# Sorted block attention with a ResMLP on one core: SyncE in program order, mixing of k and v moved to ScalarE half a batch earlier, paired scores, v sort in five pieces

## The chip, the cores and the metric

The kernel runs on one core of a Trainium2 chip. The metric is device time in microseconds (us) for one execution; less is better. The engines are named as in the profile: PE (TensorE, matmuls), PEld (its weight loads), DVE (VectorE), ACT (ScalarE), POOL (GpSimd) and SP (SyncE, which here only issues DMAs and DMA transposes). A line number such as L65 refers to the kernel before.

## The reference

Four batches of attention with 8 heads, 768 tokens and 64 channels a head feed a ResMLP block of width 512. Keys and values are mixed across 8 blocks of 96 tokens by a matrix P, made from `sort_net` by five rounds of normalisation. Attention then stays inside each block.

```python
P = sort_net
for _ in range(5):
    P = P - np.max(P, axis=-1, keepdims=True)
    P = np.exp(P)
    P = P / (np.sum(P, axis=-1, keepdims=True) + 1e-09)
    P = P / (np.sum(P, axis=-2, keepdims=True) + 1e-09)
k_sorted = np.einsum('bhij,bhjcd->bhicd', P, k_b)      # v_sorted the same
scores = scale * np.matmul(q_b, k_sb.transpose(0, 1, 2, 4, 3))
attn = softmax(scores)                                 # per block of 96
x = np.matmul(attn, v_sb)                              # to (batch, 768, 512)
a1 = alpha1 * x + beta1
tok = np.einsum('ts,bsd->btd', w_tok, a1)
u = x + lam * tok
a2 = alpha2 * u + beta2
ch = np.maximum(a2 @ w_ch1, 0.0) @ w_ch2               # 512 -> 2048 -> 512
return u + lam * ch
```

## The kernel before

**Stages.** Each batch runs in two halves (`hf`) of 384 tokens. A half has an "h" phase, the first FFN product, of 16 units of four 128x384 matmuls with a relu on ACT after each (`h_unit`, L739), and a "c" phase, the second product, of three token groups in four parts of four 128x512 matmuls (`ch_unit`, L758). The whole kernel after its head is the loop over batch, half, h units and c parts at L933 to L942. I write a place in it as (batch, half, phase slot), for instance (1,0,c4).

**What is hung beside the slots.** All other work (attention for the next batch, the token product, loads) is attached to these slots by `put` (L859) and carried out by `run` after the slot's matmuls. The table is written at L866 to L920. So PE's order is written out by hand, as a long row of FFN matmuls with pieces of the next batch in between. For batches 2 and 3, called b with p = b − 1, the places are:

- `mix_v` (L534), which mixes the values by `bigM`: (p,0,h8), h9 and h10, each two 128x512 matmuls and a copy of 1024 columns to `mixed` by DVE.
- `bounce_v` (L569) and `back_v` (L575), which write the mixed values to a scratch in DRAM (`vscr`) and gather them back into `Vs` with tokens on partitions: (p,0,h10) and (p,0,c0). Both are DMAs on SyncE.
- `mix_k` (L549), eight matmuls and four copies of 64x512 into `kT`: (p,0,h15), c1 and c4, by DVE, ACT, DVE.
- `q_cross` (L514), six DMA transposes of q on SyncE: listed at (p,0,h11). Batch 1 has `q_turn_late` (L521) in its place, which transposes on PE.
- `score` (L417), eight 96-row matmuls and an exp on ACT, and `pv` (L479), eight matmuls by `Vs`, then a reciprocal and a product on DVE: one at a time from (p,0,c8) to (p,1,h11). The first affine of a finished piece is put on the list `late` (L503) and carried out by `flush` at the next `pv`.
- `tails` (L509), which rearranges the last token rows: (p,1,h12).
- `moe_tok` (L697), the token product with u and its 16-bit copy: the first three pieces all at (p,1,c3), the others at (b,0,h0), h2 and h4. `moe_cross` (L707), three DMA transposes of u to `uT` on SyncE: (p,1,c3) and (b,0,h4). `moe_affine` (L714), which makes `a2T` from `uT` on DVE: (p,1,c7) and (b,0,h13).
- loads of the batch after next on POOL's queue (`load_kv`, `load_q`): (p,0,c11); `mix_matrix` for batches 2 and 3: (0,1,c9) and (1,1,c9).

**The head.** Before the loop (L788 to L850) batch 0 is done with other forms. k is mixed and turned on PE (`k_turn`, `k_copy`). v is rearranged in SBUF by `v_sort` (L162) into `VD`, in four pieces of 16 channels: two on DVE, one each on ACT and POOL; each `v_mix` (L401) needs eight channels. Then come scores, `pv_first` (L453), the token product (`first_mm`) and `first_turn` (L659), which ends with a matmul of one row, `rrow` by `brow`, a rank-1 term of the bias. `first_back` (L676) has three such. `fill` and `warm` (L223, L227) issue matmuls on zeros. `mgap` (L822) fills a padding column range of `Vs[0]`.

**What sets the order.** `Engine` (L55) hands each instruction to its engine and keeps it in program order; since it issues everything at L65, the profile names lines of PE, DVE, ACT and POOL as L65 and one tells them apart by tile. SyncE's DMAs are issued directly (L517, L571, L576, L710, L777, L778) and a scheduler places them: the uT transposes stand behind those of q there. PSUM pool `psA` has two buffers (scores, pv, mixing), `psB` four (FFN and token products). `qn`, `qT`, `mixed` and `u16` have one buffer, `raw` and `kT` two.

## Time and profile before

| | us |
|---|---|
| median of 5 runs | 271.66 (271.05 to 272.94) |
| profiled execution | 271.66 |
| its span on the core | 269.9 |

The granted PE clock is 1.00 of full speed over the span. The span is cut into 40 slices of 6.75 us in the page's second part; a digit is the busy share in tenths:

```profile
ACT  3577766325886003453674003453583014505600
POOL 8767205401671185303560825303100837032000
DMA  6999999999999953249399952159200323112012
GB/s 104 207 203 193 207 207 217 187 141 191 133 182 168 118 118 93 44 117 155 80 185 165 112 143 63 39 125 149 82 0 0 80 58 78 22 39 78 0 41 78
```

ACT goes to zero or near it in every second product, since its work is the relu of the first. DMA traffic is dense for the first 95 us and light later.

SyncE's own list around the end of the first batch, start and duration of each group of issues:

```profile
53.94 3.91 SPq L710 DMA_TRANSPOSE uT<-u  x3
58.92 1.15 SPq L571 DMA_DIRECT2D vscr<-mixed  x2
63.16 0.35 SPq L777 DMA_DIRECT2D out_dram<-ost  x1
63.56 0.40 SPq L778 DMA_DIRECT2D out_dram<-ost  x1
64.47 0.33 SPq L576 DMA_DIRECT2D Vs<-vscr  x1
```

These are the u transposes of half 1 of batch 0, the bounce of batch 1's values, an output store, and the gather of those values.

### The profile page before, as it was taken

Reading aid. Unit: us, or ns where it says so; the run is one execution under the profiler, and the core shown is the slowest. Engines: PE = TensorE matmul, PEld = TensorE weight load, DVE = VectorE, ACT = ScalarE, POOL = GpSimd, SP = SyncE. Lnnn points to the kernel's source line nnn. Section 1 sums busy time; section 2 is a strip of 40 time slices with the busy share of each in tenths; the row PEclk is TensorE's granted clock in tenths of the full one; section 3 lists DMA queues with packets and bytes.
Section 4 is the critical chain, followed back from the end, with each engine's and each line's share of the span. In section 5 each row is a group of like instructions: output and inputs, shape, how many; then the busy total and the mean of one; then the engine's idle time right before and its main releaser. Section 6 shows DMA issues by size and latency. Waiting matters only on the chain.

```text
span 269.9 us, 5367 instructions
## 1 busy us (share of the span) xinstructions
PE 256.3 (95%) x2151; PEld 138.8 (51%) x2165; DVE 175.1 (65%) x363; ACT 116.2 (43%) x220; POOL 98.4 (36%) x104
## 2 busy tenths in 40 slices
PE   7978999999999999999999979999999999999993
PEld 3456665455555444554555435554565445545552
DVE  5798957978378968676778728666878765121032
ACT  3577766325886003453674003453583014505600
POOL 8767205401671185303560825303100837032000
PEclk9999999999999999999999999999999999999999
DMA  6999999999999953249399952159200323112012
GB/s 104 207 203 193 207 207 217 187 141 191 133 182 168 118 118 93 44 117 155 80 185 165 112 143 63 39 125 149 82 0 0 80 58 78 22 39 78 0 41 78
DMA packets 67372, 31.04 MB, mean 115 GB/s; under 512 B 56642, under 2 KB 63058, under 8 KB 67348
## 3 DMA queue, kind: packets, MB, share of 16 engines
q0 software_dynamic: 26352, 15.34, 40.9%
q1 hardware_dynamic: 40900, 15.30, 32.5%
q8 instruction: 17, 0.28, 0.4%
q14 instruction: 7, 0.06, 0.1%
q10 hardware_dynamic: 96, 0.07, 0.1%
HBM read 32.79 MB, written 8.65 MB: 154 GB/s over the span
## 4 chain that ended last, share of the span: by engine, by line
PE 76%; DVE 11%; DMA 7%; issue 3%; POOL 1%; SPq 1%; DVEq 0%; POOLq 0%
PE h_ps L65 29%; PE ch_ps L65 24%; PE tok_ps L65 10%; DMA v<-in_v_dram 4%; DVE a L65 4%; PE x_ps L65 4%; DVE x L65 3%; PE sc_ps L65 2%; DVE ost L65 2%; DMA uT<-u 2%; PE kmix_ps L65 1%; PE v_ps L65 1%; PE mix_ps L65 1%; DVE vd L65 1%; DMA out_dram<-ost 1%
## 5 line engine op out<-in xcount | busy, mean ns | idle before, releaser
L65 PE MATMUL h_ps<-a2T,W1p 128*128 128x384 bf16 x512 | 96.1, 326 | 2.0 <-DVE a2T L65 2.0
L65 ACT ACTIVATE hTa<-h_ps 128x384 bf16<-128x384 f32 x96 | 46.9, 493 | 93.2 <-PE h_ps L65 93.1
L65 POOL TENSOR_TENSOR ost<-ost,u 128x512 f32<-128x512 f32 x21 | 26.6, 1266 | 114.6 <-DVE ost L65 108.2
L65 PE MATMUL ch_ps<-W2p,hTa 128*128 128x512 bf16 (+1 forms) x287 | 67.3, 370 | 0.6
L65 PEld LDWEIGHTS <-W1p 128*128 128x128 bf16 x512 | 47.2, 98 | 34.2 <-issue 3.5
L65 PEld LDWEIGHTS <-hTa 128*128 128x128 bf16 x300 | 28.4, 98 | 29.0
L65 DVE TENSOR_TENSOR ost<-ch_ps,lamB 128x512 f32<-128x512 f32 (+1 forms) x25 | 16.7, 669 | 37.7 <-PE ch_ps L65 34.5
L65 ACT ACTIVATE et<-sc_ps 96x768 f16<-96x768 f32 (+1 forms) x32 | 25.9, 809 | 12.9 <-PE sc_ps L65 12.9
L65 POOL TENSOR_TENSOR u<-toktmp,x 128x512 f32<-128x512 f32 x18 | 29.1, 1633 | 5.1 <-DVE toktmp L65 5.1
L65 PE MATMUL tok_ps<-a,w_tokT 128*128 128x512 f16 x126 | 29.7, 379 | 0.1
L65 PE MATMUL ch_ps<-W2p,hTb 128*128 128x512 bf16 (+1 forms) x99 | 24.8, 370 | 0.1
L65 DVE TENSOR_TENSOR toktmp<-tok_ps,lamB 128x512 f32<-128x512 f32 x21 | 14.4, 687 | 9.6 <-PE tok_ps L65 8.3
L65 DVE TENSOR_TENSOR u<-toktmp,x 128x512 f16<-128x512 f32 (+1 forms) x24 | 19.5, 824 | 0.7
L65 PEld LDWEIGHTS <-w_tokT 128*128 128x128 f16 x126 | 12.2, 98 | 14.3 <-issue 0.6
L65 ACT ACTIVATE hTb<-h_ps 128x384 bf16<-128x384 f32 x32 | 15.7, 490 | 8.0 <-PE h_ps L65 7.6
L65 POOL DMA_DIRECT2D qn<-in_q_dram x18 | 16.0, 913 | 6.2 <-DMA raw<-in_v_dram 6.2
L65 DVE CAST kT<-kmix_ps 64x512 f16<-64x512 f32 x20 | 14.2, 711 | 4.5 <-PE kmix_ps L65 3.0
L65 DVE TENSOR_TENSOR x<-x_ps,rcb 96x512 f16<-96x512 f32 x24 | 16.5, 687 | 0.8
L65 DVE TENSOR_SCALAR a2T<-uT,ab2col 128x384 bf16<-128x384 f16 x28 | 10.4, 434 | 9.3 <-DMA uT<-u 9.3
L65 PE MATMUL x_ps<-Vs,et 96*128 96x65 f16 (+4 forms) x288 | 14.4, 195 | 2.1 <-DVE x L65 1.2
L65 PEld LDWEIGHTS <-et 96*128 96x128 f16 (+4 forms) x288 | 12.5, 100 | 7.0 <-DVE x L65 2.8
L65 ACT CAST kT<-kmix_ps 64x512 f16<-64x512 f32 x16 | 11.4, 714 | 9.7 <-PE kmix_ps L65 9.5
(116 smaller groups left out, 241.7 us busy)
## 6 DMA issues: line engine op xcount, KB each, us to landing
out_dram<-ost SPq DMA_DIRECT2D x23, 192.0 KB, 2.2
raw<-in_v_dram POOLq DMA_DIRECT2D x6, 384.0 KB, 8.0
raw<-in_k_dram POOLq DMA_DIRECT2D x6, 384.0 KB, 10.3
qn<-in_q_dram POOLq DMA_DIRECT2D x18, 128.0 KB, 10.6
vscr<-mixed SPq DMA_DIRECT2D x6, 384.0 KB, 3.7
Vs<-vscr SPq DMA_DIRECT2D x3, 768.0 KB, 7.6
W1p<-in_moe_w_ch_dram POOLq DMA_DIRECT2D x4, 512.0 KB, 13.1
W2p<-in_moe_w_ch_dram POOLq DMA_DIRECT2D x4, 512.0 KB, 17.5
```

The lines of the kernel that those rows point to most:

```text
L65: ins = getattr(self.eng, name)(*args, **kwargs)
```

## The change

- SyncE's DMAs also go through `Engine`, so SyncE issues in the order in which the program lists them.
- For batches 2 and 3, `mix_v` and `mix_k` move half a batch ahead, into the second product of (p−1,1): mix_v at c1, c2, c3, mix_k at c4, c6, c8, all copies by ACT; bounce at c4, gather at c10. Their q transposes are listed at (0,1,h13) for batch 2 and (1,1,h8) for batch 3; in the built program they stand on SyncE behind the stores of the half before.
- Scores and pv of batches 2 and 3 come in pairs: at (p,0,h15), c1, c3, c6, c8, c11, (p,1,h1), h4. `flush` runs one slot after a pv pair and takes the list from its front.
- tails at h8; moe_tok at c0, c1, c2, moe_cross at c2, moe_affine at c6.
- Loads of batch 3 at (1,0,c0); `mix_matrix` at (0,0,c6) and (1,0,h12). q turns of batch 1 stay where they are.
- The head: v sort as ACT 8 + 8 channels, DVE 16, POOL 16 + 16; `brow` and `rrow` become 128 rows, zero but for row 0, so that the rank-1 matmuls run over 128 rows; two fills in `score` go, warm counts 4 and 2 become 3 and 3; the `mgap` copy moves ahead of the k copies; three copies change between DVE and ACT.

```diff
+    sp = Engine(nc.sync)
...
+    brow = att.tile([128, C], F16, name="brow", tag="uT", bufs=2)
+    rrow = att.tile([128, 384], F16, name="rrow", tag="uT", bufs=2)
...
+    dve.memset(brow[:].bitcast(FT), 0.0)
+    dve.memset(rrow[:].bitcast(FT), 0.0)
...
-    def v_sort(n, eng):
...
+    def v_sort(lo, hi, eng):
+        eng(VD[:, lo:hi, 0:HB], v8[:, :, lo:hi].rearrange("p t d -> p d t"))
...
-    v_sort(3, pool.tensor_copy)
+    v_sort(16, 32, pool.tensor_copy)
     for g in range(4):
+        if g == 1:
+            v_sort(48, 64, pool.tensor_copy)
         pool.dma_start(W1p[:, :, g * 512:(g + 1) * 512], w1v[:, :, g * 512:(g + 1) * 512])
-    brow = att.tile([1, C], F16, name="brow", tag="uT", bufs=2)
-    rrow = att.tile([1, 384], F16, name="rrow", tag="uT", bufs=2)
-    pool.tensor_tensor(brow[:], bet1[:], lam1[:], ALU.mult)
+    pool.tensor_tensor(brow[0:1, :], bet1[:], lam1[:], ALU.mult)
...
-        if b == 0 and g == 3:
-            fill(ps[:, 0, :], 1)
...
-        flush()
+        if b == 1:
+            flush()
...
-            late.pop()()
+            late.pop(0)()
...
-        nc.sync.dma_start_transpose(
+        sp.dma_start_transpose(
             qT_of[b][:, :, kt * 128:(kt + 1) * 128], qn_of[b][:, kt, :, :].rearrange("p h d -> p (h d)"),
         )
...
-    warm(4)
+    warm(3)
     mix_values(0, psb)
     prep_scales()
+    dve.tensor_copy(Vs[0][:, :, D:GRP], mgap[:].unsqueeze(2).to_broadcast([128, H * NB, GRP - D]))
...
-    warm(2)
+    warm(3)
...
-    v_sort(0, copy)
+    v_sort(0, 8, act.copy)
+    v_sort(8, 16, act.copy)
     score(0, 0, 0, psa)
     k_copy(0, 3, kp3, 0, copy)
-    k_copy(0, 3, kp3, 1, act.copy)
+    k_copy(0, 3, kp3, 1, copy)
     score(0, 0, 1, psa)
-    v_sort(1, copy)
+    v_sort(32, 48, copy)
...
-    v_sort(2, act.copy)
...
+    pairs = [("s", 0), ("s", 2), ("p", 0), ("s", 4), ("p", 2), ("s", 6), ("p", 4), ("p", 6)]
...
+            for n in range(3):
+                put(p - 1, 1, "c", 1 + n, lambda b=b, n=n: mix_v(b, n, act.copy))
+                put(p - 1, 1, "c", 4 + 2 * n, lambda b=b, n=n: mix_k(b, n, (act.copy,) * 4))
+            put(p - 1, 1, "c", 4, lambda b=b: bounce_v(b))
+            put(p - 1, 1, "c", 10, lambda b=b: back_v(b))
+            for kt in range(NT):
+                put(p - 1, 1, "h", (13 if b == 2 else 8), lambda b=b, kt=kt: q_cross(b, kt))
+            if b + 1 < B:
+                put(p, 0, "c", 0, lambda b=b: load_kv(b + 1), lambda b=b: load_q(b + 1))
+            for (kind, n), at_ in zip(
+                pairs, ((0, "h", 15), (0, "c", 1), (0, "c", 3), (0, "c", 6), (0, "c", 8), (0, "c", 11), (1, "h", 1), (1, "h", 4)),
+            ):
+                if kind == "p":
+                    put(p, at_[0], at_[1], at_[2] + 1, flush)
+                for i in range(2):
+                    f = (lambda b=b, n=n + i: score(b, n // 2, n % 2, psa)) if kind == "s" else (lambda b=b, n=n + i: pv(b, n // 2, n % 2))
+                    put(p, *at_, f)
...
-            put(p, 1, "c", 4 if b == 1 else 3, lambda b=b, kt=kt: moe_tok(b, kt, psb))
-        put(p, 1, "c", 4 if b == 1 else 3, lambda b=b: moe_cross(b, 0))
-        put(p, 1, "c", 8 if b == 1 else 7, lambda b=b: moe_affine(b, 0))
+            put(p, 1, "c", 4 if b == 1 else kt, lambda b=b, kt=kt: moe_tok(b, kt, psb))
+        put(p, 1, "c", 4 if b == 1 else 2, lambda b=b: moe_cross(b, 0))
+        put(p, 1, "c", 8 if b == 1 else 6, lambda b=b: moe_affine(b, 0))
```

The other SyncE calls (`bounce_v`, `back_v`, `moe_cross`, the output stores) change from `nc.sync` to `sp` in the same way as `q_cross`.

## The prediction

> **What bounds the kernel now.** I read the page's busy shares first, then the chain of waits, then PE's own waits, and last the timeline around each stall.

> ```profile
> PE 256.3 (95%) x2151; PEld 138.8 (51%) x2165; DVE 175.1 (65%) x363; ACT 116.2 (43%) x220; POOL 98.4 (36%) x104
> PE 76%; DVE 11%; DMA 7%; issue 3%; POOL 1%; SPq 1%; DVEq 0%; POOLq 0%
> PE h_ps L65 <- DVE a2T L65: 2.0, 2, 1.7
> PE v_ps L65 <- DVE vd L65: 1.4, 1, 1.4
> ```

> PE (first line) is busy for 95% of the span and carries 76% of the chain, so only two things save time: fewer or cheaper matmuls, and fewer PE stalls. The last two lines (us in total, times, longest) name the largest stalls after the start-up. Busy time overstates PE's work: modelled matmul ends overlap, and a matmul held by its operand looks longer. I therefore price stalls by start-to-start distances. Lines from PE's timeline, by place:

> ```profile
> 18.91 0.90 PE L65 MATMUL v_ps<-bigV,vd 64*64 64x64 f16 x32 [1.36 <-DVE vd L65]
> 24.96 1.02 PE L65 MATMUL x_ps<-Vs,et 128*128 128x65 f16 x24 [0.60 <-DVE Vs L65]
> 32.23 0.33 PE L65 MATMUL turn_ps<-rrow,brow 1*128 1x384 f16 x1
> 62.13 0.50 PE L65 MATMUL qt_ps<-ident,qn 128*128 128x128 f16 x6
> 101.27 1.19 PE L65 MATMUL h_ps<-a2T,W1p 128*128 128x384 bf16 x4 [0.29 <-DVE a2T L65]
> 127.68 0.34 PE L65 MATMUL sc_ps<-qT,kT 64*128 64x96 f16 x8
> 127.95 1.04 PE L65 MATMUL ch_ps<-W2p,hTa 128*128 128x512 bf16 x4
> 134.26 0.43 PE L65 MATMUL x_ps<-Vs,et 96*128 96x65 f16 x8 [0.49 <-DVE x L65]
> 161.53 1.19 PE L65 MATMUL h_ps<-a2T,W1p 128*128 128x384 bf16 x4 [1.71 <-DVE a2T L65]
> ```

> Read: two waits in the head (18.91, 24.96), two at the entry of a half's first FFN product (101.27, 161.53), one on a late softmax division (134.26). SyncE's list shows why a2T is late:

> ```profile
> 86.15 8.34 SPq L517 DMA_TRANSPOSE qT<-qn  x6
> 95.67 3.81 SPq L710 DMA_TRANSPOSE uT<-u  x3
> 146.63 8.20 SPq L517 DMA_TRANSPOSE qT<-qn  x6
> 156.02 3.83 SPq L710 DMA_TRANSPOSE uT<-u  x3
> ```

> Six q transposes hold SyncE for 8.3 us right ahead of the uT transposes that a2T needs.

> [...] 156 GB/s at 52 to 56 us, mostly POOL's loads, and 125 at 56 to 60.5 once SyncE's bounce runs too. [...] the same 128x768 v copy on DVE took 2.12 us beside POOL's 1.49 us copy and 0.81 us later. [...] the exps took 0.81. [...]

> **The change, part by part** (against the profiled span 269.9; the run took 271.66, 1.76 outside the span, and equals the median).

> *1. Head.* The v sort in five pieces puts two half pieces on ScalarE [...], one full on DVE, two on POOL. The first v_mix waited 1.36. ScalarE's half piece can be ready 17.6 to 17.9, v having landed at 16.64; but the exps queue behind two pieces, and scores have two PSUM buffers. I give −0.7 here and −0.3 for later v-mix evictions. Moving the 0.49 us gap copy of Vs to an idle stretch of DVE removes the x_ps wait, −0.6. So batch 0's first x_ps starts near 23.4 instead of 24.96. The gap copy now delays the first k copies by 0.49; if the later warm matmul didn't cover this, a third of the head's gain would be lost. The dropped fills (0.33, 0.31) count nothing: there x evictions on DVE set the pace. Four rank-1 turns get 128 rows instead of one; the one-row matmul took 0.27 start to start and slows its neighbour. I estimate 0.2 each, −0.8 (bounds 0 and −1.2); three in first_back, −0.45 (0 to −0.6). The two added memsets run in DVE's idle start. Natural lead before q's turn: 1.6 + 0.8 + 0.45 = **2.85**.

> *2. What the lead meets.* q_turn of batch 1 needs its q pieces. The last load was issued at 50.77 and took 9.5 us: landed 60.2. POOL's queue is busy with weights and loads throughout the head (about 205 GB/s), so a faster PE doesn't bring it forward. Worse, SyncE's uT transposes (53.94) and the 768 KB bounce (58.92, 3.7 us) move up by the lead, beside that q. If the bounce takes its whole time ahead of q, q lands at 63.9, 1.8 us behind today's turn; if it costs nothing, the whole lead passes. I take 61.5, PE's turn at 61.6 instead of 62.13: **−0.5** (bounds +1.8, −2.85).

> *3. uT stalls.* At 101.27 PE lost 0.47 idle plus 0.38, because the first four h matmuls took 1.03 instead of 0.65 while a2T pieces came: 0.85. At 161.53: 1.88 + 0.38 = 2.26. Sum **3.1**. After: mix_v and mix_k for batches 2 and 3 move into the preceding (p−1, 1) second product, about 1.3 + 1.35 us of PE work, which moves PE's arrival 2.65 later relative to this chain; batch 3's q transposes go onto SyncE some 8 us sooner, tok matmuls up to three slots sooner. Batch 2's q transposes still stand ahead of uT(1,0) (about 86 to 94), but a2T is only needed near 102. New in-order waits on SyncE: behind a held q transpose stand an output store, uT and then the v bounce; q of batch 2 is loaded a phase ahead, and its buffer is free when the last score of batch 1 is done, as now. Bound if in-order SyncE still holds uT: gain 0. I take −3.1. ScalarE's new load in that product: [...] 12 x 0.714 (kT row) [...], where it was busy for 0.38 and 0.50. The last copy ends about 1.8 after the phase; the first relu result is needed about 3.2 after. That cover is 1 to 2 us; without it each us late is a us on PE, twice.

> *4. Late softmax division.* 133.60 to 134.26 = 0.66, once each for batches 2 and 3: **−1.3**. DVE loses its mix copies there and pv's are further apart. In a pair the second waits for a PSUM buffer instead; the slots leave about 4 us between pairs, and exp (0.81 x 2) or division (about 1.1 x 2) fits. Bounds 0, −1.3.

> *5. Pairs.* A single score costs 0.27 start to start at 127.68, and stretches the next ch group by about 0.1 [...]: 0.38. A pair: about 0.45 + 0.10. Saved 0.2 x 8 pairs = **−1.6** (bounds 0, −2.4).

> Sum −0.5 − 3.1 − 1.3 − 1.6 = −6.5: span 263.4, time **265.2**. PE's matmul work otherwise stays; the earlier batch-3 loads (about 112 instead of 132) run in a stretch of light DMA use.

> **Rivals.** (a) *The lead passes.* q lands as now or a little sooner, and the turn starts with PE's lead: −2.85 in place of −0.5, span 261.05, time 262.8. For: the DMA share of the windows falls from 2.38 at 52 to 56 us to 1.77 at 56 to 60.5, so some room is there. Against: 9.5 us of landing is queue time. (b) *The stalls come back.* ScalarE's copies reach into the relus, or SyncE's order holds uT, so the 3.1 isn't gained: 268.3. For: three waits with 1 to 2 us of cover each; against: arrival moves 2.65 later. That the change fails to do what it says belongs here: if q's transposes start when they did, as batch 2's nearly do, only mixing shifts. (c) *Slower: q starves at its turn.* If the bounce and the 768 KB gather (L576, 7.6 us to landing) both run ahead of q's tail, q lands near 62 + 7.6, about 69.7 (PE's turn 7.6 late); PE, ready at 59.3, idles 10 us [...]. [...] It decides from a turn later than 68.1 [...], where the other gains are eaten. Against: the gather waits for the bounce, which began as q nearly landed.

> **How the numbers follow.** Main 0.52, (a) 0.18, (b) 0.19, (c) 0.11. A change under 0.5%, 1.36 us, is what measurement can't tell. (c) is slower; the tail of (b) with the pairs and division also worth nothing, about a third of it, is within 0.5%: same 0.06. Faster 0.83, slower 0.11. The main case alone spans 263.3 to 267 by its unknowns (turn +1.8 or −1.9, half of pairs). The range reaches (a)'s 262.8 with half a microsecond below, and (b) with half above: 262.2 to 268.8; most of (c) and the outer tails of (a) and (b) stay out.

> **What would show it.** Head: first x_ps near 23.4, no wait on Vs. Step 2: start of q's turn, 61.6 against 59.3 or over 66, and its releaser. Step 3: no a2T wait on PE at the h entries, ScalarE near 70% in those second products, no relu waits afterwards. Step 4: no DVE x release for PE. Step 5: sc_ps groups of 16, near 0.45. The forecast is wrong if PE waits for kT, et or PSUM inside the new pairs, or if span falls without these waits falling.

## The result and the profile after

| | before | after |
|---|---|---|
| median, us | 271.6 (47 runs, 270.8 to 274.2) | 270.87 (28 runs, 268.89 to 274.29) |
| profiled execution, us | 271.66 | 270.57 |
| its span, us | 269.9 | 268.8 |

The ratio is 0.9959, 95% interval 0.9943 to 0.9975: about 1.1 us faster, where 6.5 were forecast. Medians here and below are of all runs, ratios only of those within 1.5% of the fastest, so six of the 28 runs here stay out of the ratio, and below one run of 906.78 us among the 20 of the head alone. The page's busy shares and chain, and PE's slices:

```profile
PE 254.1 (95%) x2147; PEld 140.5 (52%) x2163; DVE 152.0 (57%) x343; ACT 133.9 (50%) x242; POOL 100.2 (37%) x105
PE   8997799999999999996799999999999999999993
PEclk9999999999999999999799999999999999999999
...
PE 73%; DMA 15%; POOL 4%; DVE 4%; issue 1%; SPq 1%; ACT 0%; DVEq 0%; POOLq 0%
```

The mixing has moved from DVE (175 to 152 us) to ACT (116 to 134). DMA on the chain has doubled, from 7% to 15%: a load of weights, W2p, now has 6 points of it and had at most 1 before, and uT went from 2 to 5. PE has a dip in two slices, about 121 to 134 us, in its clock too in the second of them, that the kernel before didn't have. The list of waits names it:

```profile
DVE a2T L65 <- DMA uT<-u: 20.3, 6, 9.1
PE sc_ps L65 <- DVE x L65: 3.8, 2, 3.4
PE v_ps L65 <- issue: 1.1, 1, 1.1
PE x_ps L65 <- issue: 0.9, 1, 0.9
```

PE no longer waits for a2T at an h entry: the 2.0 us row of before is gone. In its place stands one place where PE waits for DVE (3.4 and 0.3 us, behind which DVE itself waited 9.1 us for one uT), and two "issue" waits in the head. PE's, DVE's, SyncE's and POOL's timelines around the first, one fence each:

```profile
122.79 2.76 PE L65 MATMUL ch_ps<-W2p,hTa 128*128 128x512 bf16 x11
128.99 0.50 PE L65 MATMUL sc_ps<-qT,kT 64*128 64x96 f16 x8 [3.45 <-DVE x L65]
129.83 0.50 PE L65 MATMUL sc_ps<-qT,kT 64*128 64x96 f16 x8 [0.34 <-DVE x L65]
130.27 1.89 PE L65 MATMUL ch_ps<-W2p,hTb 128*128 128x512 bf16 x4
```

```profile
126.26 1.25 DVE L65 TENSOR_SCALAR a2T<-uT,ab2col 128x384 bf16<-128x384 f16 x4 [9.06 <-DMA uT<-u]
127.42 0.68 DVE L65 TENSOR_TENSOR ost<-ch_ps,lamB 128x512 f32<-128x512 f32 x1
128.02 0.19 DVE L65 RECIPROCAL rcb<-x_ps 96x8 f32<-96x8 f32 x1
128.25 0.69 DVE L65 TENSOR_TENSOR x<-x_ps,rcb 96x512 f16<-96x512 f32 x1
```

```profile
105.28 0.32 SPq L65 DMA_DIRECT2D Vs<-vscr  x1
105.70 5.55 SPq L65 DMA_DIRECT2D out_dram<-ost  x2
111.35 4.15 SPq L65 DMA_TRANSPOSE uT<-u  x3
```

```profile
112.98 1.10 POOL L65 DMA_DIRECT2D raw<-in_v_dram  x2
114.07 1.05 POOL L65 DMA_DIRECT2D raw<-in_k_dram  x2
115.08 3.58 POOL L65 DMA_DIRECT2D qn<-in_q_dram  x4
```

Read from the bottom: POOL starts the loads of batch 3 at 112.98, during the three uT transposes of (1,1) that SyncE began at 111.35. The timed transpose, the last of the three, took 12.2 us to land, where 2.4 was the median before:

```profile
DMA to landing us min/median/max: 12.2/12.2/12.2
```

The packets of the trace show how. The first two transposes had moved their 1024 packets of 256 B by 114.65. The 512 packets of the third run from 118.36 to 125.45; in the kernel before, where no packet of a load starts beside them, the third took 0.75 us (111.67 to 112.42). From 118 to 123, 165 of them start beside 154 packets of the loads of k and v, which have 6144 B and took 0.47 us each by the median: about one for one. Why none starts between 114.65 and 118.36 the trace doesn't show.

DVE reached the affine of that uT, at (1,0,h13), and stood there for 9.06 us with the output product and two softmax divisions behind it, though this a2T isn't needed before 136. The pv results therefore kept both `psA` buffers, and PE waited 3.45 us for one. The line of four ch matmuls at 130.27 takes 1.89 us where such a group took 1.03 at 121.42. The granted clock is 0.50 from 128.99 to 132.40, so 0.76 in the window of 126 to 133:

```profile
120.00:126.00 6.00, 5.50 (x52) 2.75 (x52) 0.00 (x0) 1.50 (x2) 1.00 (x2) 1.00 1.79 160
126.00:133.00 7.00, 3.67 (x24) 1.64 (x25) 5.65 (x14) 1.61 (x2) 1.26 (x1) 0.76 1.89 124
```

DVE is busy for 0.00 us from 120 to 126, while DMA runs at 160 GB/s.

### The profile page after: what moved, and what is told of

Read it like the earlier page. It is cut to its first block, busy times and chain, and to the rows that moved or that the text cites. A ratio compares the mean times of both kernels' runs of the same rounds, so it can differ in the third digit from the quotient of the medians.

```text
span 268.8 us, 5354 instructions
## 1 busy us (share of the span) xinstructions
PE 254.1 (95%) x2147; PEld 140.5 (52%) x2163; DVE 152.0 (57%) x343; ACT 133.9 (50%) x242; POOL 100.2 (37%) x105
## 4 chain that ended last, share of the span: by engine, by line
PE 73%; DMA 15%; POOL 4%; DVE 4%; issue 1%; SPq 1%; ACT 0%; DVEq 0%; POOLq 0%
PE ch_ps L65 28%; PE h_ps L65 27%; PE tok_ps L65 10%; DMA W2p<-in_moe_w_ch_dram 6%; DMA uT<-u 5%; DMA v<-in_v_dram 4%; PE x_ps L65 2%; PE sc_ps L65 2%; DVE a L65 2%; PE kmix_ps L65 2%; PE mix_ps L65 1%; POOL vd L65 1%; POOL W1p L65 1%; DVE ost L65 1%; SPq L65 1%
## 5 line engine op out<-in xcount | busy, mean ns | idle before, releaser
L65 PE MATMUL h_ps<-a2T,W1p 128*128 128x384 bf16 x512 | 91.8, 326 | 0.1
L65 ACT ACTIVATE hTa<-h_ps 128x384 bf16<-128x384 f32 x96 | 46.8, 493 | 53.9 <-PE h_ps L65 53.8
L65 PE MATMUL ch_ps<-W2p,hTa 128*128 128x512 bf16 (+1 forms) x285 | 67.7, 371 | 0.8
L65 PEld LDWEIGHTS <-W1p 128*128 128x128 bf16 x512 | 48.3, 98 | 32.3 <-issue 0.3
L65 POOL TENSOR_TENSOR ost<-ost,u 128x512 f32<-128x512 f32 x21 | 26.6, 1268 | 84.5 <-DVE ost L65 61.6
L65 PEld LDWEIGHTS <-hTa 128*128 128x128 bf16 x300 | 28.5, 99 | 29.4 <-issue 0.8
L65 POOL TENSOR_TENSOR u<-toktmp,x 128x512 f32<-128x512 f32 x18 | 29.7, 1653 | 35.2 <-DVE toktmp L65 35.2
L65 DVE TENSOR_TENSOR ost<-ch_ps,lamB 128x512 f32<-128x512 f32 (+1 forms) x25 | 16.7, 668 | 44.8 <-PE ch_ps L65 43.4
L65 ACT ACTIVATE et<-sc_ps 96x768 f16<-96x768 f32 (+1 forms) x32 | 24.9, 810 | 24.8 <-PE sc_ps L65 24.8
L65 PE MATMUL tok_ps<-a,w_tokT 128*128 128x512 f16 x126 | 30.3, 379 | 0.1
L65 ACT CAST kT<-kmix_ps 64x512 f16<-64x512 f32 x32 | 22.9, 716 | 10.1 <-PE kmix_ps L65 9.8
L65 DVE TENSOR_TENSOR toktmp<-tok_ps,lamB 128x512 f32<-128x512 f32 x21 | 14.5, 690 | 21.6 <-PE tok_ps L65 20.3
L65 PE MATMUL ch_ps<-W2p,hTb 128*128 128x512 bf16 (+1 forms) x99 | 25.5, 381 | 0.1
L65 DVE TENSOR_SCALAR a2T<-uT,ab2col 128x384 bf16<-128x384 f16 x28 | 10.3, 429 | 20.3 <-DMA uT<-u 20.3
L65 PEld LDWEIGHTS <-w_tokT 128*128 128x128 f16 x126 | 12.3, 98 | 14.0 <-DVE a L65 0.5
L65 ACT ACTIVATE hTb<-h_ps 128x384 bf16<-128x384 f32 x32 | 15.7, 491 | 7.5 <-PE h_ps L65 7.2
L65 POOL DMA_DIRECT2D qn<-in_q_dram x18 | 16.0, 913 | 4.4 <-DMA raw<-in_v_dram 4.4
L65 DVE TENSOR_TENSOR u<-toktmp,x 128x512 f16<-128x512 f32 (+1 forms) x24 | 17.0, 719 | 0.7
L65 DVE TENSOR_TENSOR x<-x_ps,rcb 96x512 f16<-96x512 f32 x24 | 16.5, 687 | 0.8
L65 PEld LDWEIGHTS <-et 96*128 96x128 f16 (+4 forms) x288 | 11.9, 100 | 5.7 <-DVE x L65 1.6
L65 PEld LDWEIGHTS <-hTb 128*128 128x128 bf16 x100 | 9.6, 99 | 10.1 <-issue 0.5
L65 PE MATMUL x_ps<-Vs,et 96*128 96x65 f16 (+4 forms) x288 | 13.0, 195 | 1.9 <-issue 0.9
```

Source lines behind the costliest of these rows:

```text
L65: ins = getattr(self.eng, name)(*args, **kwargs)
```

## The experiments

The first theory: the loads at (1,0,c0) collide with uT, and DVE's order passes the delay to PE. The rival: SyncE in program order holds uT behind bounce and gather. The next four kernels were measured together, beside the kernel before at 271.72.

**Loads back where they were.**

```diff
-                put(p, 0, "c", 0, lambda b=b: load_kv(b + 1), lambda b=b: load_q(b + 1))
+                put(p, 0, "c", 11, lambda b=b: load_kv(b + 1), lambda b=b: load_q(b + 1))
```

> The changed kernel with one step undone: the loads of batch 3 go back from (1,0,c0) to (1,0,c11). Theory (the loads collide with the uT transposes of (1,1), DVE waits in order for uT, so the softmax divisions are late and PE waits for a PSUM buffer): DVE's wait on uT falls from 9.1 us to about 3, PE's wait of 3.45 us in the score pair and the clock dip go, time about 5 to 6 us below the changed kernel, near 265. Rival (SyncE in program order holds uT behind bounce and gather): uT lands late still, time stays near 270.5.

268.1 (266.02 to 271.34), ratio 0.9838 (0.9775 to 0.99). The stall at 129 and the dip go, but another wait comes. SyncE's and PE's timelines:

```profile
146.76 9.12 SPq L65 DMA_TRANSPOSE qT<-qn  x6
155.97 3.83 SPq L65 DMA_TRANSPOSE uT<-u  x3
```

```profile
161.57 1.19 PE L65 MATMUL h_ps<-a2T,W1p 128*128 128x384 bf16 x4 [2.21 <-DVE a2T L65]
```

q of batch 3 now arrives too late for its earlier transposes, and with SyncE in order uT(2,0) stands behind them. This is the wait of before over again, and it costs more: the six token matmuls behind it take 2.12 us where they took 1.46 in the kernel before, the mean granted clock of the profiled execution is 0.990 (0.999 with the loads at c4 below), and PE loses 4.4 us there against the kernel with the loads at c4. DVE's longest wait on uT stays long too (9.6 us), but at this later place, where only the h entry follows it; the forecast of about 3 was wrong. So the early load serves the early q transposes, and it is only too early by a few slots.

**Loads between the two.** The same edit, with slot 4 in place of 11.

> As the changed kernel, with the loads of batch 3 at (1,0,c4): after uT of (1,1) has been issued and, without the loads, landed. Theory: same as with c11, near 265, and k, v, q of batch 3 are there some 8 us sooner; no new wait. Rival (any load in that second product delays what SyncE moves): a wait on Vs or uT near 125 to 135 remains, 268 or more.

264.83 (264.7 to 265.09), ratio 0.9746 (0.9713 to 0.9779). Later kernels are set against this 264.83; those of the two later groups were measured beside the kernel before at 271.94 (SyncE free, pairs, first form of more instructions, no matmuls on zeros) and 271.46 (second form, old head). uT of (1,1) lands in 2.5 us, and DVE's longest wait on uT is 3.5. PE's timeline at the same score pair has no wait, and its list of waits holds none for a2T or at these pairs for x. The landing of uT, and PE's timeline:

```profile
DMA to landing us min/median/max: 2.5/2.5/2.5
```

```profile
124.97 0.51 PE L65 MATMUL sc_ps<-qT,kT 64*128 64x96 f16 x16
125.41 1.04 PE L65 MATMUL ch_ps<-W2p,hTb 128*128 128x512 bf16 x4
```

**The collision kept, DVE's order changed.**

```diff
-        put(b, 0, "h", 13, lambda b=b: moe_affine(b, 1))
+        put(b, 0, *(("c", 11) if b == 1 else ("h", 13)), lambda b=b: moe_affine(b, 1))
```

> The changed kernel with the loads left at (1,0,c0), but DVE's affine of uT(1,1) moved from (1,0,h13) to (1,0,c11), behind the softmax divisions of those slots. Theory: uT still lands near 126, 12 us after its issue, but DVE no longer stands before it, PE's 3.45 us wait goes, time near 265 as well. Rival (the loads slow something else, the gather or k and v themselves): PE still stalls in the second product of (1,0), time stays near 270.

266.89 (266.75 to 269.87), ratio 0.9845 (0.9787 to 0.9903). Loads and transposes stand as in the changed kernel and the transpose still takes 10.9 us, yet the wait at the pair is gone. What is left is a wait of 1.02 us at the entry of (1,1) on the a2T that now comes last:

```profile
125.53 0.51 PE L65 MATMUL sc_ps<-qT,kT 64*128 64x96 f16 x16
132.46 1.84 PE L65 MATMUL h_ps<-a2T,W1p 128*128 128x384 bf16 x8 [1.02 <-DVE a2T L65]
```

Its span, 264.9, is 2.0 above that of the loads at c4: 1.4 at this entry, and 0.6 in a head that is the same in both. The two runs together show both links of the chain: the loads make uT late, and DVE's order makes that expensive. The rival on bounce and gather falls, since both stand where they did.

**The head alone**, put into the kernel before.

> The kernel before with the head part of the change alone (v sort in five pieces, rank-1 terms over 128 rows, fills, warms and the gap copy). Theory (PE's instruction stream is refilled every 256 PE instructions [...], and this rules from 16 to 29 us): first FFN relu no earlier than before within 0.3 us, time 271.6 within 0.5. Rival (the v sort's own pieces are late, but rank-1 and gap copy still give something): 0.8 to 1.5 below the kernel before.

270.96, ratio 0.9974 (0.9958 to 0.9989), about 0.7 us faster than the kernel before: between what the two theories gave. The first relu ends 0.79 earlier in the profiled runs (39.59 against 40.37), while in the changed kernel, with the same head, it ends at 40.38. So the head is worth something, but the amount varies from execution to execution. One part lies at the very start: PE's twelve start-up matmuls took 5.17 us in the changed kernel's trace and 4.21 in that of before, and the first q transposes start at 6.30, 6.00 and, with the head alone, 6.04. PE's timeline of the changed kernel shows the other part:

```profile
17.89 0.93 PE L65 MATMUL v_ps<-bigV,vd 64*64 64x64 f16 x32
20.90 0.40 PE L65 MATMUL v_ps<-bigV,vd 64*64 64x64 f16 x13
22.44 0.47 PE L65 MATMUL v_ps<-bigV,vd 64*64 64x64 f16 x19 [1.14 <-issue]
27.15 0.84 PE L65 MATMUL x_ps<-Vs,et 128*128 128x65 f16 x18 [0.43 <-DVE x L65]
28.91 0.34 PE L65 MATMUL x_ps<-Vs,et 128*32 128x65 f16 x6 [0.93 <-issue]
```

Two waits on nothing that the profile shows, in the middle of groups whose operands are there. Start to start they cost 1.30 and 1.09 more than a matmul; in the kernel before there are gaps of 0.27 and 0.32 at the same two matmuls. Counted over matmuls and weight loads in order of start, they stand ahead of PE instruction 700 and 956 in all kernels up to here: 256 apart. The page has 2147 + 2163 PE instructions and, in its third part, 17 packets of 16 KB on an instruction queue, one for each 254:

```profile
q8 instruction: 17, 0.28, 0.4%
```

**More instructions ahead.** Both on the kernel with the loads at c4:

```diff
-    warm(12)
+    warm(7)
+    small = psa([128, 512], FT, "small_ps")
+    for _ in range(48):
+        pe.matmul(small[0:32, 0:64], wz[0:32, 0:32], wz[0:32, 0:64], start=True, stop=True)
```

> As the kernel with the loads at (1,0,c4), with five of the twelve start-up matmuls on zeros replaced by 48 small ones, which adds 86 PE instructions (weight loads and matmuls) ahead of everything. Theory (refill of PE's instructions): the two unexplained PE gaps of about 1 us move 86 PE instructions towards the start of the work, so from within the third pair of v mixes to before it, and from within the second x_ps to its start or before; their distance stays about 6.1 to 6.5 us. Rival (late v pieces, PSUM or x evictions): the gaps stay at the same matmuls.

The x_ps gap (1.63 us) moved from the 19th matmul of the second x_ps to the 17th of the first, exactly 43 matmuls or 86 instructions towards the start, and stands ahead of instruction 956 again:

```profile
32.03 0.40 PE L65 MATMUL x_ps<-Vs,et 128*32 128x65 f16 x8 [1.63 <-issue]
```

There was no gap at 700: PE came there late, at 26.0, because PE ran slower and DVE was held in this head (clock 0.88 at 16 to 30 us; the product that makes bigV took 1.69 us on DVE, where it took 0.23 in the kernel before). The time, 269.48 (266.86 to 271.62), says nothing on the gaps for that reason. The second form keeps PE active with full weights: 6 of the 12 replaced by 24 matmuls of 64 columns.

> As the kernel with the loads at (1,0,c4), with six of the twelve start-up matmuls on zeros replaced by 24 of 64 columns on full weights: 36 more PE instructions ahead of all the rest, over about the same time, with PE kept active. Theory (refill every 256 PE instructions): the gap in the second x_ps, which is ahead of its 19th matmul, moves 18 matmuls towards the start, to its beginning, and the one in the v mixes moves 18 matmuls towards the start, into the scores ahead. Rival (late operands): both stay at the same matmuls. Time within 0.7 us of 264.8 either way.

265.59 (265.05 to 269.45), ratio 0.9773 (0.975 to 0.9795), 0.76 above 264.83 where at most 0.7 was expected. PE's timeline:

```profile
20.41 0.26 PE L65 MATMUL sc_ps<-qT,kT 64*128 64x96 f16 x4
21.99 0.26 PE L65 MATMUL sc_ps<-qT,kT 64*128 64x96 f16 x4 [1.32 <-issue]
...
28.46 1.00 PE L65 MATMUL x_ps<-Vs,et 128*128 128x65 f16 x24 [1.48 <-issue]
```

Both gaps are 18 matmuls earlier, now in the middle of a group of scores and ahead of the whole second x_ps, and again ahead of instructions 700 and 956. They follow the count of instructions and not an operand.

**Without the matmuls on zeros** among the v mixes and before the first x_ps. Left out are `warm(2, psb)`, `warm(1, psb)` and the fill in `v_mix`.

> As the kernel with the loads at (1,0,c4), without the matmuls on zeros among the v mixes and before the first x_ps (7 of them, about 2.2 us of PE). Theory (refill rules there): most of the 2.2 comes back as longer gaps, 0 to 0.6 us faster than 264.8. Rival (PE rules there): 1.5 to 2.2 us faster.

264.9 (264.55 to 265.37), ratio 0.9747 (0.9715 to 0.9779): no difference from 264.83. This doesn't settle what rules there, since without them the granted clock fell to 0.76 between 16 and 30 us, and PE waited for v pieces on ACT too (1.0 us). It does show that leaving these matmuls out gains nothing here. The stretch with them (loads at c4) and without:

```profile
16.00:30.00 14.00, 11.25 (x309) 8.21 (x303) 10.39 (x22) 11.50 (x20) 10.99 (x12) 1.00 1.18 199
16.00:30.00 14.00, 11.23 (x290) 9.29 (x285) 10.88 (x21) 11.70 (x20) 10.78 (x13) 0.76 1.18 197
```

**The old head with the loads at c4.**

> The kernel with the loads at (1,0,c4), but with the head of the kernel before. If the head's gain passes to the end (as the run of the head alone, 0.7 below the kernel before, says): about 265.5. If the q turn of batch 1 or a later wait takes it back: 264.8.

265.69 (265.42 to 268.16), ratio 0.9814 (0.9768 to 0.986), 0.86 slower than 264.83 by the medians. This points to the head's gain reaching the end, but doesn't prove it: the intervals overlap, and the profiled execution happens to have a long gap with the old head as well, where the kernel before, with the same head, had 0.15 at the same matmul:

```profile
28.83 0.37 PE L65 MATMUL x_ps<-Vs,et 128*32 128x65 f16 x7 [1.25 <-issue]
```

Together with the head alone I take 0.7 to 0.9 as an estimate.

**SyncE free again**, loads at c4: `sp = nc.sync` in place of `sp = Engine(nc.sync)`.

> As the kernel with the loads at (1,0,c4), but SyncE's DMAs are placed by the scheduler again instead of in program order. If program order on SyncE carries part of the gain (it keeps the q transposes out of the way of uT): PE waits for a2T again at the entry of (1,0) or (2,0), 1 to 3 us slower than 264.8. If the gain of step 3 comes from the later arrival of PE alone: within 0.5 us of 264.8.

267.28 (266.96 to 267.62), ratio 0.9829 (0.9793 to 0.9865), 2.45 slower. SyncE's timeline and PE's:

```profile
94.80 0.54 SPq L572 DMA_DIRECT2D vscr<-mixed  x1
...
97.36 2.86 SPq L711 DMA_TRANSPOSE uT<-u  x2
100.27 0.58 SPq L572 DMA_DIRECT2D vscr<-mixed  x1
100.94 1.96 SPq L711 DMA_TRANSPOSE uT<-u  x1
```

```profile
105.24 0.90 PE L65 MATMUL h_ps<-a2T,W1p 128*128 128x384 bf16 x3 [2.26 <-DVE a2T L65]
```

The scheduler puts a half of the bounce ahead of uT(1,0) and the other half in the middle of it, and PE waits at the entry of (1,0).

**Pairs taken apart**, loads at c4: the second of each pair one slot later, flush one later too.

> As the kernel with the loads at (1,0,c4), but each pair of scores or pv of batches 2 and 3 is taken apart, the second one slot later. Step 5 of the prediction: 0.1 us [...] comes back at both sides of 16 units more, 1.6 to 3.2 us slower than 264.8, with no new wait. Rival: the pairs also cost PSUM waits, so that singles are no slower than 0.5 us.

266.47 (266.13 to 267.47), ratio 0.9809 (0.9773 to 0.9846), 1.64 slower, with no new wait in the stages concerned.

## Why the prediction was wrong

The sum came out for a kernel with the loads at c4, in part because two errors cancel (steps 1 and 2); for this kernel one sentence was wrong. **"The earlier batch-3 loads (about 112 instead of 132) run in a stretch of light DMA use"** is the step that failed. It priced a moved transfer by the average load of the stretch and didn't ask what else is issued there. The three uT transposes of (1,1) are issued at 111.35, and their operand was the next thing in DVE's row. Against the kernel with the loads at c4 the profiled runs differ by 5.9 us in span (268.8 and 262.9). Of this 0.5 is the head's variation, seen at the first relu (40.38 and 39.85), and some 5.4 the collision: 3.8 idle at the pair, the rest mostly the matmuls at a granted clock of 0.50 after it (128.99 to 132.40). A sign of being wrong that the prediction named did appear: PE waits for a PSUM buffer inside a new pair.

What the trace shows at this place: a transpose beside a fresh load took 12.2 us to land, where 2.4 was the median before, and packets of the two queues start about one for one, 33 of 6144 B and 34 of 256 B from 120 to 121 us. The prediction looked for such a collision only at q in the head, where it turned out not to matter, and its own reading there fails: the 125 GB/s at 56 to 60.5 us in the kernel before weren't due to the bounce, which is issued at 58.92. The rate was 105 before that and 161 from 58.9 to 60.5.

On the clock: after 3.45 us idle, four ch matmuls took 1.89 instead of 1.03, at a granted clock of 0.50. The other waits say that the length alone doesn't decide. After 2.21 us idle with the loads at c11, six token matmuls took 2.12 instead of 1.46 (mean granted clock of that execution 0.990). After 2.26 with SyncE free the mean is 0.999, as with the loads at c4, where no such wait is.

Step by step:

- *Step 1, head: too large.* v mixing did start at 17.89 (forecast 17.6 to 17.9), but the first x_ps came at 24.82, not 23.4. The gap ahead of it, at instruction 700, took 1.0 more than before, the one after it 0.8 more. The gap copy cost little: PE passed instruction 444 0.4 later, of which 0.3 already stood at the first q transposes. The rank-1 terms gave 0.58 (the first turn starts 0.59 later than before, the first relu ends 0.01 later) for 0.8, and those of first_back 0.21 for 0.45. The head is worth an estimated 0.7 to 0.9, not 2.85.
- *Step 2, q's landing: never reached.* PE turned q at 61.92 with no wait, by its own pace; −0.2 in place of −0.5. This error happened to make the sum smaller and so hid most of step 1's.
- *Step 3, uT stalls, −3.1: right in its amount, not in its reason.* They are gone. But I put it down first of all to PE's later arrival, which no run tries alone, and held program order on SyncE for a risk; without that order a wait of 2.26 is back at (1,0). With late loads 2.21 is back at (2,0). So the early loads, the transposes that they let start early, and program order carry this gain, and not one edit.
- *Step 3's cover on ACT: right.* kT copies ran into the first relu of (1,0), at 104.7 with the loads at c4, and PE didn't wait. In the changed kernel the copies of 1024 columns took 1.01 us each on ACT and those of kT 0.72. With the loads at c4 ACT is busy for 12.42 of 19.6 us and 10.72 of 16.2 in these two products, 63% and 66%, where near 70% was forecast.
- *Step 4, −1.3: right.* Neither 0.66 gap is left with the loads at c4.
- *Step 5, −1.6: right.* Singles cost 1.64. A pair of scores took 0.44 start to start and a single one 0.27, where 0.45 and 0.27 were forecast.
- *The rivals.* None was it. (b) named SyncE's order and ACT; (c) had the right kind, a transfer starved beside another, but at q's turn in batch 0, and how much slower it made the change was the author's estimate.

With the loads at c4 the end result is 264.83, where 265.2 was forecast for the change. That it comes so near is luck in part: the head gave less than step 1 said, and q's turn took nothing of it.

## What to carry to other kernels

When a load is moved, list what other queues issue at its new place and which engine waits for it in order, and price the slowest of these. The average DMA share of the stretch didn't tell this here. An instruction that waits for a DMA and isn't urgent belongs behind urgent ones on its engine. And of several edits that look redundant (early loads, early transposes, program order) each may be what the others stand on.

## What the runs showed of the hardware

Where PE has one gap ahead of instruction 700 and one ahead of 956 of its stream, they are 256 apart, and with 36 more instructions ahead both came at the same count, 18 matmuls earlier. PE took 6.1 to 6.5 us for 256 instructions there in the kernel before and the changed one, with DMA at 199 to 201 GB/s. Measured as idle, the gaps were 0.15 to 1.63 us, and the same one with the same head was 0.15 in one execution and 1.25 in another. An operand wait removed ahead of such a place gave little: v mixing began 1.02 earlier than before (17.89, 18.91), and PE passed instruction 700 0.37 later (22.44, 22.07). That blocks of instructions arriving late cause the gaps is the author's theory; that a lighter DMA load would shorten them was not tried.

The 256 B packets of a transpose on SyncE's queue and the 6144 B packets of loads on POOL's started about one for one when both were at work (165 and 154 from 118 to 123 us), and the 512 small ones took 7.1 us (118.36 to 125.45) instead of the 0.75 of the kernel before.

Being busy alone didn't hold the clock: from 16 to 30 us PE was busy for 11.23 of 14 us without the matmuls on zeros and for 11.25 with them, and the granted clock was 0.76 and 1.00.
